# Six right-operand tiles at six distances from the left operands in a sigmoid attention and channel-mix kernel

## The chip, the core and the metric

The kernel runs on one core of one Trainium2 chip. The metric is the device time of one execution in microseconds (us): the median of three runs, and beside it one execution that the hardware profiler recorded. The engines are PE (TensorE: matmuls, with their weight loads shown apart as PEld), DVE (VectorE), ACT (ScalarE), POOL (GpSimd) and SP (SyncE, which issues the DMAs).

## What is computed

The reference, cut to its core (8 batches, 12 heads, 448 positions, head width 64; model width 768, hidden width 1024; all float32 or wider):

```python
scores = scale * np.matmul(q, k.transpose(0, 1, 3, 2)) - np.log(S)
attn = 1.0 / (1.0 + np.exp(-scores))
x = np.matmul(attn, v)                  # heads side by side: (8, 448, 768)
x_prev = x shifted by one position
xk = mu_k * x + (1.0 - mu_k) * x_prev
xr = mu_r * x + (1.0 - mu_r) * x_prev
k = np.maximum(xk @ w_k, 0.0)
v = k * k @ w_v
r = 1.0 / (1.0 + np.exp(-(xr @ w_r)))
out = r * v
```

## The kernel before, in words

The program has two parts. The attention comes first: 48 pairs of heads, whose scores (line 363), score tails (line 372) and weighted sums (lines 398, 408 and 422) run on PE, with the sigmoid on ACT (line 387). Its result goes through `gather` (line 428) to DRAM as the two mixed inputs `xr_d` and `xk_d`.

Then come three large products, the stages R_, K_ and V_ (by w_r, w_k and w_v). Each is done by Strassen's scheme with seven half-size products (p = 0 to 6, taken in `ORDER`), in four column groups (`PAIRS`), three of 512 columns and one of 256. Precision is kept by splitting each operand into a high and a low float32r part; `multiply` (line 635) issues, for each tile of depth t, high by high, high by low and low by high (line 653), all into one PSUM bank by the matmul of line 655. In the 256-column group the high and low parts lie side by side in one tile, so a 512-column matmul takes both, and a 256-column one follows for the low left part (line 651).

The **left operands** (weights, loaded into the array ahead of each matmul) lie in seven tiles `slots`, each [128, 3072] float32r, 12,288 bytes a partition. A left operand is 128 columns, 512 bytes, and starts a multiple of 512 bytes into its slot, since the widths in `CW` (384, 512, 384) are multiples of 128.

The **right operands** (which stream through the array) lie in eight pairs taken in turn (line 525 and 526): six tiles `rr`, each [128, 2, 512] float32r with the high part in the first half and the low part 2048 bytes later, and two pairs that the attention leaves, `qh` with `ql`. `operand` (line 577) fills the next pair: ACT writes the high part (line 584), DVE subtracts to get the low part (line 585). A pair is written again eight operands later, once the matmuls that read it are done.

The order of all engines is written by a planner, `Plan`: every operation has a cost and a due time, and a simulated run gives the order in which the instructions are issued. Addresses play no part in it.

Two pools hold the tiles in SBUF. `base` grows from low addresses: slots, rr, ys, wraw, wbits, wexpo. `apool` lies at the high end: the attention's tiles, with four gaps between them that no instruction touches. Modulo 512 bytes, counted from the left operand of the matmul to its right one, the built program has these distances before the change:

| matmuls | left | right | distance, bytes modulo 512 |
|---|---|---|---|
| products, line 655 | slots (slot0 at byte 2272) | rr (rr0 at byte 88,288) | 0 for all six |
| products, line 655 | slots | qh, ql (qh0 at byte 167,392) | 256 for all four |
| scores, line 363 | kh, kl (kh0 at 175,776) | qh, ql | 320 |
| weighted sums, lines 398, 422 | vn (vn0 at 148,896) | pf, pt (pf0 at 181,984) | 320 or 64, by the chunk of vn |

Of the kernel before, what the change touches and what calls it, by code (L numbers as in the profile page):

```python
# [8 lines left out]
F32 = mybir.dt.float32  # L9
F32R = mybir.dt.float32r  # L10
# [98 lines left out]
def attention_then_channel_mix(  # L109
# [16 lines left out]
    P = 128  # L126
# [6 lines left out]
    T = 512  # L133
# [35 lines left out]
    NATIVE = (0,)  # L169
    ZEROS = 336  # L170

    def ring(pool, name, bufs, shape, dtype):
        return [pool.tile(shape, dtype, name=f"{name}{i}") for i in range(bufs)]

    def gap(pool, name, size):
        pool.tile([P, size // 4], F32, name=name)

    base = ctx.enter_context(tc.tile_pool(name="base", bufs=1, side="left"))
    apool = ctx.enter_context(tc.tile_pool(name="apool", bufs=1, side="right"))
# [2 lines left out]
    pscore = psc.enter_context(tc.tile_pool(name="pscore", bufs=1, space=PSUM, side="right"))  # L182

    slots = ring(base, "slot", 7, [P, 2 * WO], F32R)
    rr = ring(base, "rr", 6, [P, 2, T], F32R)
    ys = ring(base, "ys", 3, [P, T], F32)
    wraw = ring(base, "wraw", 2, [P, WP, 2], U32)
    wbits = ring(base, "wbits", 5, [P, WP], U32)
# [3 lines left out]
    knr = ring(apool, "kn", RAW, [P, T], F32)  # L192
    vnr = ring(apool, "vn", 5, [P, T], F32)
    gap(apool, "gap1", 64)
    qnr = ring(apool, "qn", RAW, [P, T], F32)
    qhr = ring(apool, "qh", LEAD, [P, T], F32R)
    qlr = ring(apool, "ql", LEAD, [P, T], F32R)
    gap(apool, "gap2", 192)
    kh = ring(apool, "kh", LEAD, [P, KW], F32R)
    kl = ring(apool, "kl", LEAD, [P, KW], F32R)  # L200
    gap(apool, "gap3", 64)
    pfr = ring(apool, "pf", PFB, [P, 2, T], F32)
    ptr = ring(apool, "pt", PTB, [P, 2, T], F32)
# [321 lines left out]
    rr = [(t[:, 0], t[:, 1], ("rr", i), ("rr", i, "lo")) for i, t in enumerate(rr)]  # L525
# [283 lines left out]
```

## Time and profile before

| what | value |
|---|---|
| median of three runs | 805.14 us (804.46 to 805.19) |
| the profiled execution | 805.27 us |
| its span, first to last instruction | 803.0 us |
| PE busy | 798.6 us, 99% of the span |
| weight loads (PEld) | 597.8 us |
| DVE busy | 639.4 us |
| ACT busy | 498.0 us |
| matmuls of the products, line 655 | 2553 |

The page gives busy times of one profiled execution, the chain of waits that ended last, and groups of instructions. A group's row reads: line, engine, operation, output tile <- input tiles, shapes and count, then busy time and mean duration in ns, then the idle time ahead of it and what ended it. Matmuls overlap each other, so a group's mean is a latency; the pace is read from the starts in the timeline, whose rows begin with start and duration in us. A row of the view by stretches of time gives, after the stretch and its length, the busy time of PE, PEld, DVE, ACT and POOL, each with its count of instructions, then the granted clock, the DMA share and GB/s.

### The profile page before, as it was taken

What the parts mean: (1) busy time and instruction counts of PE and PEld (TensorE: products, weight loads), DVE (VectorE), ACT (ScalarE), POOL (GpSimd) and SP (SyncE); (2) the same over time, 40 slices, a digit from 0 to 9 for tenths busy, and PEclk for the clock granted to TensorE, in tenths of its full rate; (3) what the DMA queues carried; (4) which work ended last, traced back from release to release, by engine and by line L of the source; (5) the groups of instructions that cost most, each with busy time, mean ns of one, the idle gap of its engine ahead of it and who ended that gap; (6) DMA issues with size and microseconds to landing.
All of it is one profiled execution on the core that took longest, in us unless ns stands there. A gap on an engine that the chain in (4) does not pass through costs nothing.

```text
span 803.0 us, 14330 instructions
## 1 busy us (share of the span) xinstructions
PE 798.6 (99%) x4927; PEld 597.8 (74%) x4927; DVE 639.4 (80%) x1207; ACT 498.0 (62%) x868; POOL 3.0 (0%) x33
## 2 busy tenths in 40 slices
PE   9999999999999999999999999999999999999998
PEld 4555555555556888888888888888888888888887
DVE  4898889898898998898987974669597585677955
ACT  5788888877776555668776464668773434345431
POOL 0000000000000000000000000000000000000000
PEclk9999999999999999999999999999999999999999
DMA  8878888698887977667877782445675564457505
GB/s 289 266 252 275 270 268 276 231 320 302 298 292 258 303 245 227 218 222 256 279 264 221 241 258 87 171 145 159 217 243 173 179 185 131 131 173 256 174 22 177
DMA packets 105193, 179.75 MB, mean 224 GB/s; under 512 B 11936, under 2 KB 58656, under 8 KB 105120
## 3 DMA queue, kind: packets, MB, share of 16 engines
q1 hardware_dynamic: 104832, 178.44, 67.8%
q8 instruction: 39, 0.64, 0.3%
q10 hardware_dynamic: 288, 0.39, 0.1%
q14 instruction: 34, 0.28, 0.1%
HBM read 109.06 MB, written 69.73 MB: 223 GB/s over the span
## 4 chain that ended last, share of the span: by engine, by line
PE 99%; DMA 0%; DVE 0%; issue 0%
PE pb L655 69%; PE av L398 13%; PE sc L363 10%; PE av L422 2%; PE sc L372 2%; PE av L363 2%; PE av L408 1%; DMA qn<-in_q 0%; DVE vn L705 0%
## 5 line engine op out<-in xcount | busy, mean ns | idle before, releaser
L655 PE MATMUL pb<-rr,slot 128*128 128x512 f32 (+1 forms) x1908 | 440.5, 379 | 0.0
L655 PEld LDWEIGHTS pb<-rr,slot 128*128 128x128 f32 x1908 | 347.7, 188 | 68.8 <-issue 0.8
L655 PE MATMUL pb<-qh,slot 128*128 128x512 f32 (+1 forms) x468 | 154.8, 375 | 0.0
L398 PE MATMUL av<-pf,vn 64*64 64x448 f32 x1104 | 117.4, 540 | 0.0
L387 ACT ACTIVATE pf<-sc 128x896 f32<-128x896 f32 x120 | 103.9, 958 | 3.2 <-PE sc L363 3.2
L655 PEld LDWEIGHTS pb<-qh,slot 128*128 128x128 f32 x468 | 86.1, 188 | 16.1
L398 PEld LDWEIGHTS av<-pf,vn 64*64 64x64 f32 x1104 | 41.1, 132 | 57.1 <-issue 35.9
L655 PE MATMUL pb<-ql,slot 128*128 128x512 f32 (+1 forms) x177 | 68.4, 387 | 0.0
L584 ACT CAST rr<-ys 128x512 fp32r<-128x512 f32 (+1 forms) x56 | 30.6, 567 | 36.1 <-PE pb L655 34.5
L363 PE MATMUL sc<-qh,kh 64*128 64x448 f32 x236 | 45.4, 381 | 0.0
L713 ACT COPY pb<-pb 128x512 f32<-128x512 f32 x40 | 22.9, 572 | 34.1 <-PE pb L655 32.9
L432 ACT COPY xx<-av 128x448 f32<-128x448 f32 x48 | 23.3, 539 | 32.1 <-PE av L398 23.1
L363 PE MATMUL sc<-ql,kh 64*128 64x448 f32 (+1 forms) x236 | 43.2, 363 | 0.0
L363 PE MATMUL sc<-qh,kl 64*128 64x448 f32 x236 | 42.7, 359 | 0.0
L433 DVE TENSOR_TENSOR dx<-xx 128x448 f32<-128x448 f32 x48 | 29.9, 622 | 15.9 <-ACT xx L432 15.8
L585 DVE TENSOR_TENSOR rr<-pf,rr 128x512 fp32r<-128x512 f32 (+1 forms) x40 | 23.1, 608 | 22.3 <-ACT rr L584 22.2
L655 PEld LDWEIGHTS pb<-ql,slot 128*128 128x128 f32 x177 | 33.3, 188 | 6.7
L585 DVE TENSOR_TENSOR rr<-ys,rr 128x512 fp32r<-128x512 f32 (+1 forms) x56 | 33.6, 620 | 4.7 <-ACT rr L584 4.6
L585 DVE TENSOR_TENSOR rr<-vn,rr 128x512 fp32r<-128x512 f32 (+1 forms) x48 | 29.6, 626 | 8.0 <-ACT rr L584 7.9
L363 PEld LDWEIGHTS sc<-qh,kh 64*128 64x128 f32 x236 | 22.1, 184 | 18.2 <-issue 16.2
L584 ACT CAST rr<-vn 128x512 fp32r<-128x512 f32 (+1 forms) x48 | 26.9, 570 | 12.3 <-PE pb L655 10.2
L717 ACT COPY pf<-pb 128x512 f32<-128x512 f32 x28 | 16.4, 587 | 29.1 <-PE pb L655 28.4
(161 smaller groups left out, 1078.1 us busy)
## 6 DMA issues: line engine op xcount, KB each, us to landing
vn<-in_v SPq DMA_DIRECT2D x48, 224.0 KB, 4.7
xr_d<-mr SPq DMA_DIRECT2D x48, 224.0 KB, 4.6
xk_d<-mk SPq DMA_DIRECT2D x48, 224.0 KB, 4.7
kn<-in_k SPq DMA_DIRECT2D x47, 224.0 KB, 3.8
qn<-in_q SPq DMA_DIRECT2D x47, 224.0 KB, 4.1
wraw<-in_moe_w_k SPq DMA_DIRECT2D x12, 512.0 KB, 6.0
wraw<-in_moe_w_v SPq DMA_DIRECT2D x16, 384.0 KB, 3.7
k_d<-pt SPq DMA_DIRECT2D x23, 256.0 KB, 3.5
```

What stands on the lines that cost most here:

```text
L363: nc.tensor.matmul(sc[u][:, h, :w], kk[half[h], c * P:(c + 1) * P], qq[half[h], :w], start=e == 0, stop=e == len(pairs) - 1, skip_group_ch ...
L372: nc.tensor.matmul(sc[u][half[m % 2], h, :S], kn[m % RAW][half[h], KW:], qn[m % RAW][half[h], :], start=True, stop=True)
L387: op(ACT, 815, at, lambda: nc.scalar.activation(f, sc[u][:, :, :S], AF.Sigmoid, bias=NEG_LOG_S, scale=SCALE), R, K, opens=opens)
L398: nc.tensor.matmul(av[m % 2][half[h], :w], vn[m % 5][half[r], h * NC + c, :], pfr[(m * NC + c) % PFB][half[r], h, :w], start=(turn, c) == ...
L422: nc.tensor.matmul(av[r][half[h], :w], vn[(n + h) % 5][half[r], 2 * NC, :], ptr[n // 2 % PTB][half[r], h, :w], start=False, stop=stop, ski ...
L432: op(ACT, act(S), at - 1, lambda: nc.scalar.copy(x[:, 1:], av[n % 2][:, :S]), [AV[n % 2]], [X])
L433: op(DVE, dve(S), at, lambda: nc.vector.tensor_sub(d, x[:, 1:], x[:, :S]), [X], [G])
L584: op(ACT, act(w, True), at, lambda: nc.scalar.copy(hi, y[:, :w]), [Y], [H], gate=True)
L585: op(DVE, dve(w), at, lambda: nc.vector.tensor_sub(lo, y[:, :w], hi), [Y, H], [L])
L655: nc.tensor.matmul(b[0][:, :m], l, r[:, :m], start=p in (0, 4) and e == 0, stop=e == len(terms) - 1, skip_group_check=True)
L713: op(ACT, act(T), at, lambda: nc.scalar.copy(y(), x()), [X], [Y])
L717: op(ACT, act(T), at, lambda: nc.scalar.copy(u, y()), [Y], [U])
```

## The change

The six `rr` tiles are allocated one by one, with unused tiles of 32, 96, 64, 64 and 32 bytes ahead of rr1 to rr5, and one of 224 bytes behind rr5. The distances of rr0 to rr5 from the left operands become 0, 32, 128, 192, 256 and 288 bytes modulo 512. `gap`, which allocates an unused tile, is moved ahead of `ring`. Nothing else is edited; in the built program, the tiles behind rr5 in `base` lie 512 bytes higher and those in `apool` stay where they were. Every engine has the same instructions in the same order.

```diff
-    rr = ring(base, "rr", 6, [P, 2, T], F32R)
+
+    rr = []
+    for i, size in enumerate((0, 32, 96, 64, 64, 32)):
+        if size:
+            gap(base, f"apart{i}", size)
+        rr.append(base.tile([P, 2, T], F32R, name=f"rr{i}"))
+    gap(base, "apart6", 224)
     ys = ring(base, "ys", 3, [P, T], F32)
```

with the function that it calls:

```python
    def gap(pool, name, size):
        pool.tile([P, size // 4], F32, name=name)
```

More of the change, by code (lines that the diff above doesn't have):

```diff
@@ L170, in attention_then_channel_mix, with gap @@
     ZEROS = 336
+    def gap(pool, name, size):
+        pool.tile([P, size // 4], F32, name=name)
     def ring(pool, name, bufs, shape, dtype):
         return [pool.tile(shape, dtype, name=f"{name}{i}") for i in range(bufs)]
-    def gap(pool, name, size):
-        pool.tile([P, size // 4], F32, name=name)
     base = ctx.enter_context(tc.tile_pool(name="base", bufs=1, side="left"))
```

## The prediction, made before the changed kernel was run

> **What bounds the kernel now.** I read the page's busy times first, then the chain of waits, then the instruction groups with shapes kept apart, then the timeline at four places.
>
> From the page:
>
> ```profile
> span 803.0 us, 14330 instructions
> PE 798.6 (99%) x4927; PEld 597.8 (74%) x4927; DVE 639.4 (80%) x1207; ACT 498.0 (62%) x868; POOL 3.0 (0%) x33
> PEclk9999999999999999999999999999999999999999
> ```
>
> PE is busy for 99% of the span, at the full granted clock throughout. The profiled execution took 805.27 us, so 2.27 us lie outside the span; the three timed runs have a median of 805.14 us, 0.13 us less.
>
> From the chain that ended last, in order of time, its last row:
>
> ```profile
> 247.22 552.60 PE pb L655 x2553
> ```
>
> From 247.22 us to the end the chain never leaves PE: 552.60 us of products at line 655, each waiting for nothing but the matmul ahead of it. The changed tiles are right operands of exactly these. So the question is only what one such matmul takes. The groups with their shapes give the counts:
>
> ```profile
> L655 PE MATMUL pb<-rr,slot 128*128 128x512 f32 x1722 | 419.3, 390 | 0.0
> L655 PE MATMUL pb<-qh,slot 128*128 128x512 f32 x403 | 141.6, 390 | 0.0
> L655 PE MATMUL pb<-ql,slot 128*128 128x512 f32 x173 | 67.3, 389 | 0.0
> L655 PE MATMUL pb<-rr,slot 128*128 128x256 f32 x186 | 33.7, 281 | 0.0
> L655 PE MATMUL pb<-qh,slot 128*128 128x256 f32 x65 | 14.0, 281 | 0.0
> ```
>
> The 390 ns is a latency, start to end; matmuls overlap, so the pace is read from the starts. The timeline of PE near the beginning of the products:
>
> ```profile
> 249.82 9.91 PE L655 MATMUL pb<-rr,slot 128*128 128x512 f32 x43
> 259.57 0.39 PE L655 MATMUL pb<-qh,slot 128*128 128x512 f32 x1
> 259.79 0.39 PE L655 MATMUL pb<-ql,slot 128*128 128x512 f32 x1
> ...
> 260.93 0.84 PE L655 MATMUL pb<-rr,slot 128*128 128x512 f32 x3
> ```
>
> Forty-three matmuls on rr start between 249.82 and 259.57: 9.75/43 = 226.7 ns each. The six on qh and ql that follow run from 259.57 to 260.93: 1.36/6 = 226.7 ns. That is the row on which most of this prediction rests, because the two groups differ in what the change is about. The slots are 12,288 bytes (24 times 512) and every left operand starts a multiple of 512 bytes into one, so each right tile has one distance to all of them: 0 for the six rr tiles, 256 for qh and ql. Two distances, one pace.
>
> The 256-column products, from the timeline near the end:
>
> ```profile
> 796.78 0.88 PE L655 MATMUL pb<-rr,slot 128*128 128x256 f32 x6
> 797.49 0.28 PE L655 MATMUL pb<-qh,slot 128*128 128x256 f32 x1
> ...
> 798.21 0.88 PE L655 MATMUL pb<-rr,slot 128*128 128x256 f32 x6
> 798.93 0.28 PE L655 MATMUL pb<-qh,slot 128*128 128x256 f32 x1
> ```
>
> On qh and ql (797.49 to 798.21, six of them) it is 0.72/6 = 120 ns; on rr (798.21 to 798.93) 0.72/6 = 120 ns, and 118 ns for the six before. Again no difference. Between 512 and 256 columns lie 106.7 ns, so a column costs 0.417 ns and 512 columns 213.3 ns; what is left, 13.3 ns, is a fixed part of every product matmul.
>
> The sum closes: 1722 + 403 + 173 = 2298 of 512 columns by 226.7 ns are 520.9 us, and 2553 - 2298 = 255 of 256 columns by 120 ns are 30.6 us. Together 551.5 us, against the chain's 552.60, which also holds the last matmul's latency. There is about 1 us in these products that is neither column nor fixed part, so no more than that can be won from waits.
>
> **The change part by part.** The order of instructions is the same on every engine, row for row, once the numbers that the gap tiles shift are taken off. No operation is added, removed or moved; the gaps are never written or read. What changes is addresses.
>
> The six tiles go from distance 0 to 0, 32, 128, 192, 256 and 288 bytes. rr0 keeps its distance, and rr4 gets that of qh and ql. Four distances are new to the products: 32, 128, 192, 288. The rr tiles are used in turn; counted in the order of PE, rr1, rr2, rr3 and rr5 are read by 315, 312, 316 and 325 matmuls, 1268 of the 1908 on rr. The two halves of a tile are 2048 bytes apart, so both are at the tile's distance. All gaps together are 32 + 96 + 64 + 64 + 32 + 224 = 512 bytes: tiles after them in that pool keep their place modulo 512, and the attention's tiles, in the other pool, don't move. The first 247 us can't change by this.
>
> rr0 and rr4 cost nothing: their distances are those of the two rows above. For the other 1268 matmuls I have one more distance, from the attention, where the keys (left) and queries (right) lie 320 bytes apart:
>
> ```profile
> 58.89 0.36 PE L363 MATMUL av<-ql,kh 64*128 64x448 f32 x2
> ...
> 60.69 0.37 PE L363 MATMUL sc<-ql,kh 64*128 64x448 f32 x2
> ```
>
> Nine pairs start between 58.89 and 60.69: 200 ns a pair, which is 448 columns by 0.417 = 186.7 ns and again 13.3 ns. So at 0, 256 and 320 bytes the fixed part is the same. I take it for the new distances as well: 1268 by 0 ns. Its bounds are the fixed part gone, or once more on top: 1268 by 13.3 ns = 16.9 us in either direction. I take the value in the middle because three rows have it and neither end has a row for this kind of matmul.
>
> Weight loads read the slots while the previous matmul streams its right operand, the one place where the two reads meet:
>
> ```profile
> L655 PEld LDWEIGHTS pb<-rr,slot 128*128 128x128 f32 x1908 | 347.7, 188 | 68.8 <-issue 0.8
> L655 PEld LDWEIGHTS pb<-qh,slot 128*128 128x128 f32 x468 | 86.1, 188 | 16.1
> ```
>
> A load takes 188 ns for either tile. If a new distance lengthens it, the first 226.7 - 188 = 39 ns are hidden at 512 columns. The 256-column products have less cover, but they are 186 on rr, some 124 of them on the four tiles.
>
> ACT writes the first half of a tile (line 584), DVE the second (line 585). They also get new addresses:
>
> ```profile
> L585 DVE TENSOR_TENSOR rr<-ys,rr 128x512 fp32r<-128x512 f32 x42 | 28.0, 687 | 4.7 <-ACT rr L584 4.6
> L585 DVE TENSOR_TENSOR ql<-ys,qh 128x512 fp32r<-128x512 f32 x12 | 8.1, 685 | 0.1
> L584 ACT CAST rr<-ys 128x512 fp32r<-128x512 f32 x42 | 25.2, 621 | 24.2 <-PE pb L655 22.8 <-issue 1.1
> L584 ACT CAST qh<-ys 128x512 fp32r<-128x512 f32 x12 | 7.3, 614 | 0.1
> ```
>
> 687 against 685 ns and 621 against 614 ns: nothing there follows the distance. Were DVE to slow down, what hides it is its idle time, least between 330 and 400 us:
>
> ```profile
> 330.00:400.00 70.00, 70.00 (x339) 58.97 (x339) 62.38 (x117) 50.68 (x104) 0.00 (x0) 1.00 0.72 248
> 330.00:400.00 70.00, 23.19 (x42) 1.00 0.72 248
> ```
>
> The first row has DVE busy for 62.38 of 70 us; the second, of line 585 alone, has 42 instructions in it. The 7.6 us idle give each 0.18 us before DVE has none left, a quarter of its time. Without that cover PE would wait for right operands; I put it at nothing.
>
> The sum: 803.0 + 0 us, with 2.27 us outside the span 805.3; against the median of the runs, 805.1 us. That is the forecast.
>
> **The rivals.** *The new distances save the fixed part.* For: the 13.3 ns need not belong to a matmul. The attention's float32 products, whose weights lie 320 bytes from their streams, show hardly any:
>
> ```profile
> 102.08 0.93 PE L422 MATMUL av<-pt,vn 64*64 64x448 f32 x8
> 102.83 0.56 PE L398 MATMUL av<-pf,vn 64*64 64x448 f32 x4
> ```
>
> Eight records, four at a time, take 102.83 - 102.08 = 0.75 us, 375 ns for each four; that is twice 186.7 ns and 1.6 ns. So a fixed part can be almost absent, and 13.3 ns could be a collision of the weights' reads with the stream's. The Trainium skill, page "TensorE: Matmul & The Clock Gate", section "Back-to-back issue gap", gives a warm gap of N/2.4 + 2.5 ns, for 512 columns about 216 ns; by it 11 ns of the 226.7 are a loss, and if the four tiles lost it no more the kernel would take an estimated 14 us less. Against: those records are another number format, and the product matmuls have 13.3 ns to the nanosecond at 0 and at 256, the keys at 320; a collision that depends on the distance would hardly give one number three times. Only 32 and 288, odd multiples of 32, are of a kind that no row shows. One tile's fixed part gone is 317 by 13.3 ns = 4.2 us, 800.9 us; two tiles 796.7; all four 805.1 - 16.9 = 788.2 us. Chance 0.15: 0.08 for one tile or as much in all, 0.07 for more.
>
> *The new distances bring a collision (slower).* The stream of one matmul meets the load of the next at a distance that today has no row, and the pace of that tile rises. At the price of one more fixed part, a tile costs 4.2 us: one 809.3, two 813.6, all four 822.0 us. It decides the sign from 1.6 us on, 0.2% of 805, which is about what a measurement of this kernel can tell from no change: 5 ns on one tile's 317 matmuls, or 1.3 ns on all 1268. For: four distances without a row, and 0 may be a good one. Against: 0, 256 and 320 agree, and the load has 39 ns to spare. The Trainium skill, page "SBUF — State Buffer", section "Who interferes with whom", says that TensorE has separate read ports for stream and weights and never waits on anyone; by it this rival's price is nothing. The trace agrees at 0 and 256, and shows nothing of the new four. Chance 0.2: 0.14 up to two tiles, 0.06 beyond.
>
> *It does shift the tiles, but something else on PE moves.* The roughly 1 us of the products beyond columns and fixed part could come or go. That stays inside the bound of no change.
>
> **How the numbers follow.** Forecast 805.1 us, chance 0.65, within 1 us either way; faster 0.15, slower 0.2. With the forecast's 0.65, the range takes in the slower case up to two tiles (0.14, to 813.6) and the faster one with one tile (0.08, from 800.9): 0.87 in all. By the evidence of the rows the second slower tile is the weaker part; I end the range at 811.0, between one tile and two, which leaves out about 0.2. Faster 0.15, same 0.65, slower 0.2.
>
> **What would show it.** Right: at line 655 the pace in the timeline is 226.7 ns on all six rr tiles and 120 ns at 256 columns, weight loads at 188 ns, the chain's last row at 552 to 553 us. Wrong: matmuls on two to four of the tiles start at another pace than those on rr0, rr4, qh and ql, with the excess times some 317 giving the change in time; or loads on rr take other than 188 ns; or PE shows idle time, with a wait for lines 584 or 585, which none of the terms has.

## The result, and the profile after

The changed kernel takes 813.73 us (median; 812.95 to 814.12) against 804.8 us before, a ratio of 1.0113 with a 95% interval of 1.0101 to 1.0124. It is slower by 8.9 us; the forecast was no change, and the range ended at 811.0.

In the changed kernel all lines behind the edit have numbers higher by 6: the products are line 661, the two fills of a right operand 590 and 591. From its page, span and busy times:

```profile
span 811.9 us, 14330 instructions
PE 807.5 (99%) x4927; PEld 597.6 (74%) x4927; DVE 639.4 (79%) x1207; ACT 498.1 (61%) x868; POOL 3.0 (0%) x33
PEclk9999999999999999999999999999999999999999
```

The span grew by 8.9 us, PE's busy time by 8.9 us; weight loads, DVE and ACT stayed within 0.2 us of what they were, and the clock is as it was. The last row of its chain of waits, start and length in us:

```profile
246.81 561.86 PE pb L661 x2553
```

The products took 552.60 us before and take 561.86 us now: 9.26 us more for the same 2553 matmuls. That is all of the loss; the attention ahead of them ended 0.4 us earlier. The timeline of PE near the beginning of the products:

```profile
247.79 11.79 PE L661 MATMUL pb<-rr,slot 128*128 128x512 f32 x50
259.42 0.39 PE L661 MATMUL pb<-qh,slot 128*128 128x512 f32 x1
259.65 0.40 PE L661 MATMUL pb<-ql,slot 128*128 128x512 f32 x1
...
260.80 0.84 PE L661 MATMUL pb<-rr,slot 128*128 128x512 f32 x3
```

Fifty matmuls on rr start in 259.42 - 247.79 = 11.63 us, 232.6 ns each, where it was 226.7. The six on qh and ql that follow take 260.80 - 259.42 = 1.38 us, 230 ns each, although neither their tiles nor their left operands moved. The loads of the weights are as long as before:

```profile
L661 PEld LDWEIGHTS pb<-rr,slot 128*128 128x128 f32 x1908 | 347.6, 188 | 75.6 <-issue 0.8
L661 PEld LDWEIGHTS pb<-qh,slot 128*128 128x128 f32 x468 | 86.1, 188 | 17.7
```

And nothing waits: in the stretch where DVE had the least idle time, its row is

```profile
330.00:400.00 70.00, 70.00 (x336) 58.24 (x335) 62.15 (x118) 49.47 (x101) 0.00 (x0) 1.00 0.71 244
```

PE busy for all of 70 us, with 336 matmuls started in it where it was 339, and DVE at 62.15 against 62.38 us. Outside PE's busy time the span holds 4.4 us, as before. So the loss is a slower pace of the matmuls themselves, not a wait and not DVE or ACT.

### The profile page after: what moved, and what is told of

The parts are those of the page before. It is cut to its first block, busy times and chain, and to the rows that moved or that the text cites. A ratio compares the mean times of both kernels' runs of the same rounds, so it can differ in the third digit from the quotient of the medians.

```text
span 811.9 us, 14330 instructions
## 1 busy us (share of the span) xinstructions
PE 807.5 (99%) x4927; PEld 597.6 (74%) x4927; DVE 639.4 (79%) x1207; ACT 498.1 (61%) x868; POOL 3.0 (0%) x33
## 4 chain that ended last, share of the span: by engine, by line
PE 99%; DMA 0%; DVE 0%; issue 0%
PE pb L661 69%; PE av L404 13%; PE sc L369 10%; PE av L428 2%; PE sc L378 2%; PE av L369 2%; PE av L414 1%; DMA qn<-in_q 0%; DVE vn L711 0%
## 5 line engine op out<-in xcount | busy, mean ns | idle before, releaser
L661 PE MATMUL pb<-rr,slot 128*128 128x512 f32 (+1 forms) x1908 | 447.9, 383 | 0.0
```

The costliest lines, as they stand in the source:

```text
L661: nc.tensor.matmul(b[0][:, :m], l, r[:, :m], start=p in (0, 4) and e == 0, stop=e == len(terms) - 1, skip_group_check=True)
```

## The experiments

Two things in the trace had to be told apart at first. Tiles at 32, 128, 192 and 288 might be dear by themselves (theory B). Or the mixture of distances within one chain of matmuls (those that are summed one after another into one PSUM bank) might break an even rhythm, any common distance being as good as another (theory A); the slower qh and ql spoke for it. The first four kernels were made for that. Distances below are bytes modulo 512 from the left operand to the right one; wherever not said, qh and ql stay at 256 and the tiles behind rr keep their place modulo 512. A change of `gap4` moves all tiles of `apool` together.

**All eight pairs at 32, and all at 128.** The edit for 32; for 128 the three numbers are 128, 384 and 384:

```diff
+    gap(base, "apart0", 32)
     rr = ring(base, "rr", 6, [P, 2, T], F32R)
+    gap(base, "apart6", 480)
...
-    gap(apool, "gap4", 256)
+    gap(apool, "gap4", 480)
```

> All eight right pairs (six rr, and qh with ql) at one distance, 32 bytes. Theory A, that tiles at different distances within one chain of matmuls break the even pace, and that the common distance itself does not matter: 805 us, 226.7 ns on every tile. Theory B, that a distance such as 32 is dear by itself: the matmuls on rr1 went at 233 ns in the changed kernel, so 2553 by some 6.5 ns more, 821 us.

> All eight right pairs at one distance, 128 bytes. Theory A: 805 us, 226.7 ns. Theory B: the tile at 128 went at 231.4 ns in the changed kernel, so 2553 by 4.7 ns more, 817 us.

At 32 it took 818.02 us (1.0169 of before, 1.0154 to 1.0185), at 128 818.08 us (1.0171, 1.0156 to 1.0186). The timeline of the kernel at 32:

```profile
247.76 11.13 PE L657 MATMUL pb<-rr,slot 128*128 128x512 f32 x47
258.73 0.40 PE L657 MATMUL pb<-qh,slot 128*128 128x512 f32 x1
```

10.97 us for 47 matmuls, 233.4 ns. Theory B's 821 us was 3 us too high at 32, its 817 us 1 us too low at 128. With one common distance everywhere there is nothing to mix, and the kernel is slower than with six. Theory A in its strict form falls; the distance has a price of its own.

**Only rr at 32, and only rr1 at 32.** The first is the edit above without its last line, the second `(0, 32, 480, 0, 0, 0)` as the list of gaps in the change.

> All six rr tiles at 32 bytes, qh and ql left at 256. Theory A: chains on rr alone go at 226.7 ns, the half of the chains that mix rr with qh lose some 5 ns a matmul: 1276 by 5 ns, 811 us. Theory B: 1908 matmuls on rr by 6.5 ns, 817 us, and the chains on rr alone go at 233 ns.

> Only rr1 at 32 bytes, the other five at 0. Theory A: every chain that holds rr1, some four in ten, loses about 5 ns on all its matmuls, those on other tiles too: about 5 us, 810 us. Theory B: 315 matmuls on rr1 by 6.5 ns, 2 us, 807 us, and the other tiles stay at 226.7 ns.

They took 816.7 us (1.0155, 1.0140 to 1.0170) and 807.84 us (1.0045, 1.0028 to 1.0062). The first is B's 817 us. The second is 3.7 us more than the 804.16 us of before in the same session, between the 2 us of B and the 5 us of A, so it decides for neither. B's detail, that the other tiles stay at 226.7 ns, was wrong. The timeline of the kernel with rr1 alone at 32, one chain of nine matmuls: three on qh and ql, three on rr0, three on rr1, the chain before it likewise ending on rr1:

```profile
278.82 0.39 PE L659 MATMUL pb<-qh,slot 128*128 128x512 f32 x1
279.05 0.40 PE L659 MATMUL pb<-ql,slot 128*128 128x512 f32 x1
279.28 0.39 PE L659 MATMUL pb<-qh,slot 128*128 128x512 f32 x1
279.51 1.55 PE L659 MATMUL pb<-rr,slot 128*128 128x512 f32 x6
280.90 0.39 PE L659 MATMUL pb<-qh,slot 128*128 128x512 f32 x1
```

The chain takes 280.90 - 278.82 = 2.08 us, where nine at 226.7 ns take 2.04. Three matmuls at 233.4 explain 0.02 us; the other 0.02 us fell on the six at distances 0 and 256. The kernel with all of rr at 32, and qh and ql at 256, shows it in one stretch:

```profile
247.67 12.06 PE L657 MATMUL pb<-rr,slot 128*128 128x512 f32 x51
259.57 0.40 PE L657 MATMUL pb<-qh,slot 128*128 128x512 f32 x1
...
260.96 0.86 PE L657 MATMUL pb<-rr,slot 128*128 128x512 f32 x3
```

Behind 51 matmuls on rr at 11.90/51 = 233.3 ns, the six on qh and ql take 1.39/6 = 231.7 ns each, at a distance that went at 226.7 ns before. The last rows of the chains of waits say the same for the whole run. First the kernel with rr1 at 32, then the one with everything at 32:

```profile
245.82 556.48 PE pb L659 x2553
```

```profile
246.09 566.17 PE pb L657 x2553
```

With everything at 32, 2553 matmuls cost 566.17 - 552.60 = 13.57 us, 5.3 ns each. With rr1 at 32, 315 matmuls cost 556.48 - 552.60 = 3.88 us, 12.3 ns each, so a good part of it is paid by the matmuls behind them. The trace gives the split when its 2553 starts are matched one by one with the order of the program, and each interval to the next start is compared with the same one before the change: 1.9 us lie behind starts on rr1 (6.7 ns each at 512 columns), 2.0 us behind the five matmuls that follow, and the sixth is back at its old pace. Theory A is right in this much, that a matmul behind one at a dear distance is slow too.

**Which of the two operands counts.** The next two kernels move the left operands, alone and together with the right ones:

```diff
+    gap(base, "apart0", 32)
     slots = ring(base, "slot", 7, [P, 2 * WO], F32R)
+    gap(base, "apart1", 480)
```

for the left operands alone; for all together the first of these lines, and `gap4` of 224 in place of 256, so that both pools lie 32 bytes higher as a whole.

> Only the left operands move, by 32 bytes; every right operand stays where it was. The distances become 480 for rr and 224 for qh and ql. If the distance between the two operands counts (theory B, now: each distance has a pace of its own, and 0 and 256 are the fast ones): 812 to 820 us, a pace of 231 to 234 ns on all tiles. If the place of the right operand alone counts (theory E): 805 us.

> Left and right operands all move by 32 bytes together, so every distance is as before the change and every address is new. Theory B: 805 us, 226.7 ns. Theory E, the right operand's own place counts: it is 32 bytes off as in the kernel with all right operands at distance 32, 818 us.

With the left ones moved alone it took 818.05 us (1.0172, 1.0157 to 1.0187), with all moved together 804.42 us (0.9999, 0.9990 to 1.0009). The timelines of PE, first with the left ones alone:

```profile
247.82 10.89 PE L657 MATMUL pb<-rr,slot 128*128 128x512 f32 x46
258.56 0.40 PE L657 MATMUL pb<-qh,slot 128*128 128x512 f32 x1
```

then with all of them:

```profile
247.79 11.04 PE L656 MATMUL pb<-rr,slot 128*128 128x512 f32 x48
258.67 0.39 PE L656 MATMUL pb<-qh,slot 128*128 128x512 f32 x1
```

10.74/46 = 233.5 ns against 10.88/48 = 226.7 ns. In the first kernel qh and ql never moved and the rr tiles, which lie behind the slots, went up by 512 bytes to the same place modulo 512; all of them were slow. In the second every address is new, and none was: what counts is the distance between the two operands, not the place of either. Theory E falls.

**Other common distances.** The edit of the first pair again, with other sizes.

> All eight right pairs at distance 64. Theory B: dear like 32 and 128, 812 to 820 us with one steady pace of 231 to 234 ns. The rival of the prediction that the fixed part of 13.3 ns is itself a collision, which some distance avoids: under 800 us.

> All eight right pairs at distance 96. Theory B: 812 to 820 us, a steady pace of 231 to 234 ns. The rival that some distance avoids the fixed part: under 800 us.

> All eight right pairs at distance 160. Theory B with what the other distances showed, odd multiples of 32 alike: 233.4 ns, 818 us. The rival that some distance avoids the fixed part: under 800 us.

> All eight right pairs at distance 192. Theory B: between the 228.9 ns of 64 and the 232 ns of 128, 807 to 816 us. The rival that some distance avoids the fixed part: under 800 us.

The pace is read from the timeline as above, by the start of the first row and that of the one behind it. The fences are of the kernels at 64, 96, 128, 160 and 192:

```profile
247.76 10.92 PE L657 MATMUL pb<-rr,slot 128*128 128x512 f32 x47
258.52 0.39 PE L657 MATMUL pb<-qh,slot 128*128 128x512 f32 x1
```

```profile
247.72 12.06 PE L657 MATMUL pb<-rr,slot 128*128 128x512 f32 x51
259.62 0.40 PE L657 MATMUL pb<-qh,slot 128*128 128x512 f32 x1
```

```profile
247.62 12.47 PE L657 MATMUL pb<-rr,slot 128*128 128x512 f32 x53
259.93 0.40 PE L657 MATMUL pb<-qh,slot 128*128 128x512 f32 x1
```

```profile
247.61 11.64 PE L657 MATMUL pb<-rr,slot 128*128 128x512 f32 x49
259.09 0.40 PE L657 MATMUL pb<-qh,slot 128*128 128x512 f32 x1
```

```profile
247.66 11.36 PE L657 MATMUL pb<-rr,slot 128*128 128x512 f32 x48
258.86 0.39 PE L657 MATMUL pb<-qh,slot 128*128 128x512 f32 x1
```

| distance of all pairs | median, us | ratio to before, 95% interval | pace on rr, ns |
|---|---|---|---|
| 0 (qh, ql at 256), all moved by 32 | 804.42 | 0.9999, 0.9990 to 1.0009 | 226.7 |
| 32 | 818.02 | 1.0169, 1.0154 to 1.0185 | 233.4 |
| 64 | 807.61 | 1.0038, 1.0025 to 1.0051 | 10.76/47 = 228.9 |
| 96 | 819.30 | 1.0184, 1.0167 to 1.0201 | 11.90/51 = 233.3 |
| 128 | 818.08 | 1.0171, 1.0156 to 1.0186 | 12.31/53 = 232.3 |
| 160 | 821.50 | 1.0209, 1.0194 to 1.0224 | 11.48/49 = 234.3 |
| 192 | 817.40 | 1.0159, 1.0142 to 1.0175 | 11.20/48 = 233.3 |
| 480 (qh, ql at 224), left ones moved | 818.05 | 1.0172, 1.0157 to 1.0187 | 233.5 |

None goes below 226.7 ns at 512 columns. Over all 2226 pairs of neighbouring 512-column matmuls of a trace, and not only those in the fences, the mean interval between starts is 227.2 ns at 0 and 256, 233.3 at 32, 228.9 at 64, 233.4 at 96, 232.9 at 128, 234.2 at 160, 233.1 at 192, and 233.2 with the left ones moved. The price lies in these: over the 184 neighbouring pairs of 256 columns it is 117.8 ns before and 117.5 at 32. Two distances are a little better there, 64 with 114.7 ns and 192 with 115.9.

Three of the four expectations missed. At 64 the distance is dear, but its pace by only a third as much as the others, and the time lies 4.4 us below the range given; at 160 the kernel was 3.5 us dearer than at 32, where equality was expected; at 192 it was 1.4 us above the range, nearly as dear as 128. Every distance tried with a remainder of 0 by 256 is at the one pace, and no other is.

**Half the weight load.** If the load of the next weights, 512 bytes a partition, delays the stream, half a load should delay it half as much:

```diff
-                nc.tensor.matmul(b[0][:, :m], l, r[:, :m], ...
+                c_ = P if e == 0 else P // 2
+                nc.tensor.matmul(b[0][:c_, :m], l[:, :c_], r[:, :m], ...
```

> Distances as before the change, but every product matmul except the first of a chain loads only the first 64 of its 128 weight columns (256 bytes instead of 512) and leaves out the lower half of the output rows. If the time above 213 ns comes from the weight load meeting the stream, it halves on those matmuls: 226.7 becomes some 220 ns, 790 us. If it does not come from the load: 226.7 ns, 804 us.

> The same half loads, the lower half of the output rows left out, with all right operands at distance 32. If the distance acts through the load, its price of 6.7 ns a matmul halves too: some 223 ns, 7 us above the same kernel at distance 0. If it acts on the stream alone: 233 ns, 14 us above it.

One run each: 810.92 us at distance 0 and 813.65 us at 32, beside 804.24 us before. Both expectations missed. The groups of loads show that most loads are now half as wide (first the kernel at 0, then that at 32), and the last rows of the two chains of waits follow:

```profile
L656 PEld LDWEIGHTS pb<-rr,slot 128*64 128x64 f32 x1676 | 224.2, 134 | 139.0
```

```profile
247.09 558.36 PE pb L656 x2553
```

```profile
L658 PEld LDWEIGHTS pb<-rr,slot 128*64 128x64 f32 x1676 | 224.7, 135 | 140.9
```

```profile
246.34 561.59 PE pb L658 x2553
```

A load of 134 ns in place of 188 made the products at distance 0 slower, 558.36 against 552.60 us, and those at 32 faster, 561.59 against 566.17 us. The difference between the two distances shrank from 13.57 to 3.23 us. Streams and addresses were the same; the length of the load changed, and with it the rows that a matmul writes, 64 in place of 128, so these runs can't say which of the two moved the pace. They do show that the time above 213 ns is not a sum of bytes loaded, since half the bytes made it longer at distance 0. That it depends on how load and stream fall together in time is the likeliest reading, and not shown.

The cause is settled as far as the distance goes. Why a remainder of 0 by 256 is the best one with a full load stays open; a distance finer than 32 bytes was not tried. No kernel tried is faster than the one before: its distances, 0 and 256, are the fastest found. At 64 the 256-column products gain 3.1 ns by 255, an estimated 0.8 us, and the 512-column ones lose more.

## Why the prediction was wrong, point by point

- **What bounds the kernel** was right. PE sets the time, the products' pace is the whole question, and the sum by paces closes again to 2 us: 1722 by 232.6, 576 by 230 and 255 by 120 ns are 563.6 us against 561.86. The fixed part was read too exactly, though: the 256-column pace of 120 ns is 117.8 over all 184 pairs, so 13.3 ns is not the same part of every product matmul.
- **The step that failed** is the middle value for the new distances: "So at 0, 256 and 320 bytes the fixed part is the same. I take it for the new distances as well: 1268 by 0 ns." The three rows were not three independent samples. By the runs, 0 and 256 are one case. The row for 320 came from another loop, pairs of matmuls on half the partitions, and does not seem to carry over: 64, which has the remainder of 320 by 256, costs the products 2.2 ns a matmul while the pairs showed no excess (320 itself was not tried in the products). So I had one distance, twice, and took it for a law. In place of 1268 by 0 ns the trace of the changed kernel shows 1268 by 4.6 ns, 5.9 us.
- **rr0 and rr4 "cost nothing"** was wrong too, for another reason: their own distances are free, but they stand behind dear ones. By the common-distance runs, with 288 taken as 32, the dear tiles account for (315 + 325) by 5.3 ns (32 and 288), 312 by (565.45 - 552.60)/2553 = 5.0 ns (128) and 316 by (565.48 - 552.60)/2553 = 5.0 ns (192), together 6.5 us. The two lengths are from these rows, the kernels at 128 and at 192:

```profile
247.35 565.45 PE pb L657 x2553
```

```profile
246.22 565.48 PE pb L657 x2553
```

  The other 9.26 - 6.5 = 2.7 us fell on the 1285 matmuls on rr0, rr4, qh and ql, 2.1 ns each; that qh and ql went at 230 ns is the same thing in the timeline. This split takes the common-distance prices as they stand. Interval by interval, against the trace of before, it is 5.9 us on the four dear tiles and 3.4 us on the others, 2.6 ns for each of these.
- **The slower rival** had the mechanism and the sign, with a chance of 0.2. Its price of 13.3 ns a matmul was more than twice too high, its likelier number of tiles, "up to two", half of the four that were dear, and the matmuls behind a dear tile were not in it; that the 813.6 us for two tiles lie beside the 813.73 us measured is luck, these errors cancelling. Its argument "0 may be a good one" was the right one. The 39 ns that the load had to spare did not bear on it: the loads kept their 188 ns, and the starts of the matmuls lay further apart.
- **The faster rival** fell: no distance tried goes below 226.7 ns at 512 columns, so none of them sheds the 13.3 ns over the columns' time; at 256 columns, 64 and 192 shed 2 to 3 ns, under 1 us in all. The Trainium skill's gap of about 216 ns ("TensorE: Matmul & The Clock Gate", "Back-to-back issue gap"), which the section calls that of an isolated matmul, was reached at none.
- **The rule that TensorE never waits on anyone**, with two independent read ports ("SBUF — State Buffer", "Who interferes with whom", in the Trainium skill), made the slower rival's price nothing in the prediction, and here the measurement differs: the pace follows the distance between the two operands that TensorE itself reads, 226.7 to 234.3 ns. What other engines do to it, no run here tests.
- **DVE and ACT** were right: 639.4 us and 498.1 us, as before.

## What to carry to other kernels

Where PE is the bound and every matmul has its own weights, read the pace from the starts, not from the durations or the loads, and look at the distance in bytes between left and right operands modulo 256: here, for float32r matmuls of 512 columns, a remainder of 0 was the fastest, and each of the others tried cost 1 to 3% of the pace. A tile at a bad distance also slowed the five or so matmuls behind it, so spreading tiles over several distances pays for more than the tiles that moved. And when a forecast rests on rows that agree, ask first whether they differ in the thing that is to change.

## What the runs showed of the hardware

- The pace of back-to-back float32r matmuls of 128 weights by 512 columns depended on the distance between the two operands in SBUF: 226.7 ns at a remainder of 0 by 256 bytes, 228.9 at 64, 232.3 to 234.3 at 32, 96, 128, 160, 192 and 224.
- Moving both operands by 32 bytes together changed nothing (804.42 against 804.54 us); moving either alone by 32 bytes cost 1.7%.
- A matmul at distance 32 also lengthened the intervals of the five behind it: with one tile of six there, 1.9 us fell on its own matmuls and 2.0 us on those behind.
- With a shorter weight load, 134 in place of 188 ns, and half the output rows, the matmuls at the best distance were slower (products 558.36 against 552.60 us; one run).
